# Weight conversion on three engines: a parametric relu on ScalarE, one VectorE instruction a part, V's lower half on GpSimd, and landing places inside the converted weight

## The chip, the cores and the metric

The kernel runs on one NeuronCore of one Trainium2 chip. The metric is the device time of one execution in microseconds (us). A time is given as the median of several executions. The profile is of one further execution, and its span is measured from the first to the last instruction. Engines: PE (TensorE, matmuls), PEld (its weight loads), DVE (VectorE), ACT (ScalarE), POOL (GpSimd) and SP, whose queue issues all DMAs here.

## The reference

Attention with pooled queries, then an MLP with a rational activation:

```python
# q, k, v: (4, 8, 1152, 64) float32;  w_in (512, 2048), w_out (2048, 512) float64
q_pool = q.reshape(B, H, S // 2, 2, D).mean(axis=3)          # 576 query rows
attn = softmax(scale * q_pool @ k^T)                         # 576 x 1152 per head
x = (attn @ v) laid out as (2304 tokens, 512)
h = x @ w_in
g = (a0 + a1 h + a2 h^2 + a3 h^3) / (1 + |b0| |h| + |b1| h^2 + 1e-6)
out = g @ w_out                                              # (2304, 512) float32
```

The two weights come from a random generator in float64, and nothing narrows them. The kernel therefore reads them as pairs of 32-bit words, a low word and a high word for each element, and makes float32 values of them itself. Everything is computed in pairs of float16 numbers, a high and a low part that together carry float32's precision.

## The kernel before, in words

**Attention.** A unit is a pair of heads in one batch. For each unit `prep` loads K, Q and V, finds their largest sums of squares (`pr_stat`, ACT), derives scales, and splits each operand in a high part (`pr_hi`, ACT) and a low part (`pr_lo`, DVE). V's high part is `v1`, its low part `v2`, and `v3` is a scaled copy of `v1` (`pr_v3`, DVE). K and Q are turned by a transposing DMA. A unit has nine tiles of 128 query rows. `attend` takes one tile through a fixed chain: scores on PE into the PSUM tile `sc` (`at_fill`, L718), row maxima on DVE (`at_max`, L725), their turn on PE (`at_turn`, L728), a copy of the row on ACT (`at_row`, L732), the shifted and transposed scores on PE into `st` (`at_fill2`, L741 and L742), exp on ACT (`at_exp`, L749), and the split of its result into halves on DVE (`at_split`, L757). `product` multiplies with V three tiles later (`at_pv`, L771), and `at_x` (ACT, L788) copies the result out. There are one `sc` and one `st`, so tiles follow one another closely. There are 144 tiles.

**Weights.** `weights` treats `w_in` (`wi`) and then `w_out` (`wo`) in 16 parts of 128 x 512 elements each. For every part:

- `w_load` (SP, L457) brings 512 KB of raw words into one of two buffers with the tag `raw`.
- `w_win` (POOL, L465) multiplies the high word, read as a float32, by a power of two, and writes it to `wf`, a float32 tile that holds all 16 parts.
- `w_bits` (DVE) runs three instructions: L471 moves the top three bits of the low word into the high word's place, L472 keeps only the sign of the high word, and L473 shifts `wf` left by three and ORs in these bits.
- `w_stat` (ACT, L478) sums squares.

Once all parts are there, a scale is found, and `w_hi` (ACT, L500) and `w_lo` (DVE, L504) write the two float16 parts. For `wi`, four column sums of absolute values follow (`w_abs`, `w_colsum`); they use the `raw` buffers too. When both weights are done `w_close` frees this memory and lets the first MLP chunk begin ("late").

**MLP.** A chunk is 128 tokens; 18 of them, in an order fixed by hand. `chunk` normalizes and splits the attention result; `step` does a quarter of the hidden columns: `mo_h` on PE (L913), the polynomials and the quotient on ACT, DVE and POOL (`mo_abs` L926, `mo_f` L944, `mo_e2` L948, `mo_ln` L952, `mo_rem` L971 and others), and `mo_o` on PE (L984 to L986). A chunk needs its tiles of all four units of a batch: the first chunk needs 30 tiles.

**Order.** Every operation is registered with an engine, an estimated duration in ns, a wished time and what it reads and writes. `Plan.order` runs a list scheduler forward and backward several times over these estimates and keeps the shortest result. The instructions are issued in that order, so each engine's queue has one fixed order, and an estimate that is changed can change the order of the whole program. The waits at run time are true dependences; the estimates set none.

Of the kernel before, what the change touches and what calls it, by code (L numbers as in the profile page):

```python
# [10 lines left out]
F16 = mybir.dt.float16  # L11
I32 = mybir.dt.int32
U16 = mybir.dt.uint16
BF16 = mybir.dt.bfloat16
AF = mybir.ActivationFunctionType
ALU = mybir.AluOpType
# [252 lines left out]
def kernel(  # L269
# [175 lines left out]
    def w_open():  # L445
        st["stg_cm"] = tc.tile_pool(name="stg", bufs=1)
        st["stg"] = st["stg_cm"].__enter__()

    def w_load(n, i):

        t = st["stg"].tile([P, 512, 2], I32, tag="raw", name=f"raw_{n}{i}", bufs=NRAW)
        st["raw", n, i] = t
        if n == "wi":
            src = w_in.bitcast(I32)[i // 4 * P:(i // 4 + 1) * P, (i % 4) * 1024:(i % 4 + 1) * 1024]
        else:
            src = w_out.bitcast(I32)[i * P:(i + 1) * P, :]
        nc.sync.dma_start(out=t.rearrange("p f w -> p (f w)"), in_=src)  # L457

    def w_win(n, i):
        if i == 0:
            st["wf", n] = st["stg"].tile([P, 16, 512], F32, tag="wf", name=f"wf_{n}")
        u = st["raw", n, i][:, :, 1]
        nc.gpsimd.tensor_scalar(st["wf", n][:, i, :], u.bitcast(F32), 2.0 ** -111, 1.0, ALU.mult, ALU.mult)  # L465

    def w_bits(n, i):
        mi = st["wf", n][:, i, :].bitcast(I32)
        r = st["raw", n, i]
        h = r.rearrange("p f w -> p (f w)").bitcast(U16).rearrange("p (f w) -> p f w", w=4)  # L470
        nc.vector.tensor_scalar(h[:, :, 2], h[:, :, 1], 13, None, ALU.logical_shift_right)  # L471
        nc.vector.tensor_scalar(h[:, :, 3], h[:, :, 3], 0x8000, None, ALU.bitwise_and)  # L472
        nc.vector.scalar_tensor_tensor(mi, mi, 3, r[:, :, 1], ALU.logical_shift_left, ALU.bitwise_or)  # L473

    def w_stat(n, i):

# [192 lines left out]
    def pr_lo(j, w):  # L669
        d = pairs[j]  # L670
        stt = nc.vector.scalar_tensor_tensor
        if w == "v":
            stt(pr_new(j, "v2"), d["vn"], d["ss"][:, 2:3], d["v1"][:, :, 0:D], ALU.mult, ALU.subtract)
        elif w == "q":
            stt(spq[:, KC:2 * KC, 0, :], d["qn"][:, :, 0, :], d["ss"][:, 1:2], spq[:, 0:KC, 0, :], ALU.mult, ALU.subtract)
        else:
            src = d["kn"].rearrange("p h c d -> p (h c) d")
            stt(d["spk"][:, :, 1, :], src, d["ss"][:, 0:1], d["spk"][:, :, 0, :], ALU.mult, ALU.subtract)
# [290 lines left out]
    def mo_rem(c, f):  # L969
        w = wk[c, f]  # L970
        nc.gpsimd.tensor_tensor(w["e2"], w["t"], w["e2"], ALU.subtract)  # L971
# [50 lines left out]
    def prep(j, part):  # L1022
        bb, hp, _, mode = units[j]
        o = j % 2
        if j == 0:
            at = [-100.0 + i for i in range(20)]
        else:
            p0, p1 = tile_t[first_t[j]], tile_t[first_t[j - 1]]
            sp = (p0 - p1) / 9.0
            at = [p1 + (PRM["pr0"] + PRM["pr1"] * i) * sp for i in range(20)]  # L1030
        if mode == "again":
            if hp < 2:
                for i in (0, 1) if part == 0 else (2, 3, 4):
                    add("dma", cost(256 * op_cols(i)), at[6], lambda i=i: pr_again(j, i), r=[("kept", bb, hp, i)], w=[("set", o, i)], seq=["seqag"])
                if part == 0:
                    add("dma", (625, 820, 624), at[7], lambda: pr_kb(j), r=[("set", o, 1)], w=[("set", o, 5)])
            return
        if part == 1:
            add("act", 1240, at[14], lambda: pr_hi(j, "v"), r=["vn", ("ss", j)], w=[("set", o, 2)])
            add("dve", 1500, at[15], lambda: pr_lo(j, "v"), r=["vn", ("ss", j), ("set", o, 2)], w=[("set", o, 3)])  # L1040
            add("dve", 370, at[16], lambda: pr_v3(j), r=[("set", o, 2)], w=[("set", o, 4)])
            if mode == "first" and hp < 2:
                for i in range(5):
                    add("dma", cost(256 * op_cols(i)), at[17], lambda i=i: pr_save(j, i), r=[("set", o, i)], w=[("kept", bb, hp, i)], seq=["seqsv"])
            return
        add("dma", cost(128 * 4608), at[0], lambda: pr_load_k(j), w=["kn"])
        add("dma", (1400, 1640, 449), at[0], lambda: pr_load_q(j), w=["qn"])
        add("dma", cost(128 * 4608), at[1], lambda: pr_load_v(j), w=["vn"])
        add("pool", 1500, at[6], lambda: pr_pool(j), w=["qn"])
        add("act", 1146, at[6], lambda: pr_stat(j, 0), r=["kn"], w=[("st", j), "spk"])  # L1050
        add("act", 700, at[6], lambda: pr_stat(j, 1), r=["qn"], w=[("st", j), "spk"])
        add("act", 1146, at[6], lambda: pr_stat(j, 2), r=["vn"], w=[("st", j), "spk"])
        chain(at[7], half_exp(lambda: pairs[j]["st"]), w=[("st", j)])
        bank = over_all(at[7], lambda: pairs[j]["st"], (0, 1, 2, 2), 3, [("st", j)], False)
        on_dve, on_pool = pr_scale(j)
        chain(at[7], on_dve(bank), r=["ALLB"], w=[("ss", j)], bank=B_ALL)
        chain(at[7] + 1.0, on_pool, r=[("ss", j)], w=[("esc", j)])
        for i in range(2):
            add("pool", 400, at[7] + 1.0, lambda i=i: pr_sv(j, i), r=[("ss", j)], w=[("sv", bb, hp, i)])
        for i, w in enumerate(("k", "q")):  # L1060
            add("act", 1240, at[8 + 2 * i], lambda w=w: pr_hi(j, w), r=[w + "n", ("ss", j)], w=["sp" + w])
            add("dve", 820 if w == "q" else 1650, at[9 + 2 * i], lambda w=w: pr_lo(j, w), r=[w + "n", ("ss", j)], w=["sp" + w])
            add("dma", T_TR2, at[9 + 2 * i], lambda w=w: pr_tr(j, w), r=["sp" + w], w=[("set", o, 0 if w == "q" else 1)])
            if w == "k":
                add("dma", (625, 820, 624), at[10], lambda: pr_kb(j), r=[("set", o, 1)], w=[("set", o, 5)])

    def attend(t):
        j, slot = tiles[t]
        o = j % 2
        s = time_of(t)  # L1070
        jp = prep_of[j]
        E = ("E", t % NE)
        M = ("M", t % NM)
        wide = slot == 8
        add("pe", (650, 1100) if wide else (490, 960), s, lambda: at_fill(t), r=[("set", o, 0), ("set", o, 1)], w=["S"], seq=["seqS"], bank=B_S)
        add("dve", 1330, s + 0.6, lambda: at_max(t), r=["S"], w=[M], bank=B_S)
        add("pe", (60, 128), s + 2.1, lambda: at_turn(t), r=[M], w=["TURN"], seq=["seqM"], bank=B_TURN)
        add("act", 230, s + 2.3, lambda: at_row(t), r=["TURN", ("set", o, 0)], w=[("row", t)], bank=B_TURN)
        add("pe", (1150, 2304) if wide else (1010, 2304), s + 2.7, lambda: at_fill2(t), r=[("row", t), ("set", o, 0), ("set", o, 1), ("set", o, 5)], w=["T"], seq=["seqT"], bank=B_T)
        add("act", 1300, s + 3.9, lambda: at_exp(t), r=["T", ("esc", jp)], w=[E], seq=["seqE"], bank=B_T)  # L1080
        add("dve", 780, s + 5.3, lambda: at_split(t), w=[E], seq=["seql"])

    def product(g, host):
        j, bb, hp, slot, _ = at_rows(g)
# [7 lines left out]
    def weights(n, s0):  # L1092
        for i in range(16):
            s = s0 + PRM["ws"] * i
            raw, wf = ("raw", i % NRAW), ("wf", i)
            add("dma", cost(128 * 4096), s, lambda i=i: w_load(n, i), w=[raw], seq=["raw"])
            add("pool", 700, s + 4, lambda i=i: w_win(n, i), r=[raw], w=[wf], seq=["win"])
            add("dve", 2300, s + 4, lambda i=i: w_bits(n, i), w=[wf, raw])
            add("act", 615, s + 6, lambda i=i: w_stat(n, i), r=[wf], w=[("wst", n, i)])
        s = s0 + 16 * PRM["ws"] + 2  # L1100
        add("dve", 100, s, lambda: w_max1(n), r=[("wst", n, i) for i in range(16)], w=[("m1", n)])
# [1 line left out]
        bank = over_all(s, lambda: st["m1", n], (0,), 1, [("m1", n)], True)  # L1103
        chain(s, w_scale(n, bank), r=["ph"], w=[("sw", n)])
        for i in range(8):
            wf = [("wf", 2 * i), ("wf", 2 * i + 1)]
            add("act", 1141, s + PRM["wl"] * i, lambda i=i: w_hi(n, i), r=wf + [("sw", n)], w=[(n, 0, i)])
            add("dve", 1330, s + PRM["wl"] * i, lambda i=i: w_lo(n, i), r=wf + [("sw", n), (n, 0, i)], w=[(n, 1, i)])
        s += 8 * PRM["wl"]
# [62 lines left out]
    def step(p, f):  # L1172
# [16 lines left out]
        add("pool", 1330, u + PRM["m_f"], lambda: mo_e2(c, f), r=[A], w=[E2])  # L1189
        add("act", 700, u + PRM["m_ln"], lambda: mo_ln(c, f), r=[E2], w=[A])  # L1190
        add("act", 620, u + PRM["m_ln"], lambda: mo_r(c, f), w=[A])
        add("dve", 750, u + PRM["m_ghi"], lambda: mo_ghi(c, f), r=[T, A], w=[G], seq=["seqG"])
        add("dve", 770, u + PRM["m_d1"], lambda: mo_d1(c, f), r=[G], w=[E2])
        add("pool", 1400, u + PRM["m_rem"], lambda: mo_rem(c, f), r=[T], w=[E2])
        add("dve", 800, u + PRM["m_glo"], lambda: mo_glo(c, f), r=[A], w=[G, E2, T])

        po = "po_t" if last else "po"
        wos = [("wo", l, x) for l in range(2) for x in range(8)]
# [66 lines left out]
```

## Time and profile before

| what | value |
|---|---|
| median of 3 runs (lowest, highest) | 953.59 us (952.13, 958.34) |
| profiled execution: time, span | 954.2 us, 952.4 us |
| busy: PE, DVE, ACT, POOL | 816.0, 794.1, 602.2, 446.0 us |
| mean granted TensorE clock | 0.939 |

The profiled execution takes 954.2 us with the 1.8 us around its span, and lies 0.6 us above the median. A row of the groups gives line, engine, operation, output<-input, shapes, count, then busy time and mean ns of one, then the engine's idle time just before these instructions with what ended it. A row of the windows gives the busy time of each engine in one stretch, then the granted clock and the DMA share.

### The profile page before, as it was taken

The page shows a single profiled execution, that of the slowest core. Times are in us where ns is not written, and L with a number is a line of the kernel's source. Part 1 is how long each engine was busy: PE and PEld are TensorE (multiplying, and loading weights), DVE is VectorE, ACT ScalarE, POOL GpSimd, SP SyncE. Part 2 cuts the span into 40 slices and gives each one's busy share as a digit, 9 for nine tenths or more (in the row PEclk, how much of TensorE's full clock was granted, in tenths as well). Part 3 has the DMA queues.
Part 4 walks back from the last instruction along what each step waited for, and adds up shares of the span by engine and source line. Part 5 has one row for each costly group of instructions (what it writes and reads, how often), then busy time and mean ns, then how long its engine had stood idle before and what let it go on. Part 6 is the DMA issues. An engine that isn't in the chain of part 4 may idle for free.

```text
span 952.4 us, 27847 instructions
## 1 busy us (share of the span) xinstructions
PE 816.0 (86%) x12196; PEld 650.4 (68%) x12196; DVE 794.1 (83%) x1075; ACT 602.2 (63%) x905; POOL 446.0 (47%) x482
## 2 busy tenths in 40 slices
PE   0477675545999999989998999989899998999998
PEld 0266554444877877768777788668677777887764
DVE  7698797888999897868999888869888897996765
ACT  4466595456876676657675686557667755775453
POOL 4212103342565553436764553425856544645765
PEclk9998777766999999979999999989999999999999
DMA  5784518462340060652150061445736120430100
GB/s 188 199 182 132 139 35 215 155 177 60 60 103 13 13 149 13 139 124 49 24 140 23 13 150 21 130 117 138 141 125 149 38 40 24 113 113 13 35 12 23
DMA packets 121338, 88.79 MB, mean 93 GB/s; under 512 B 96769, under 2 KB 98817, under 8 KB 121217
## 3 DMA queue, kind: packets, MB, share of 16 engines
q1 hardware_dynamic: 121216, 87.02, 37.0%
q8 instruction: 95, 1.56, 0.7%
q14 instruction: 27, 0.21, 0.1%
HBM read 49.24 MB, written 8.87 MB: 61 GB/s over the span
## 4 chain that ended last, share of the span: by engine, by line
PE 55%; DVE 12%; ACT 6%; POOL 6%; DMA 5%; issue 3%; SPq 1%; POOLq 0%; DVEq 0%; ACTq 0%
PE ph_h L913 15%; PE po L984 5%; PE po L986 5%; PE po L985 5%; PE st L741 5%; PE st L742 5%; PE sc L718 5%; PE sc L771 5%; PE st L771 4%; DVE mt L725 2%; DMA raw_wo<-in_moe_w_out_dram 2%; POOL e L944 1%; DMA k<-spk 1%; POOL e L948 1%; DVE E L757 1%
## 5 line engine op out<-in xcount | busy, mean ns | idle before, releaser
L749 ACT ACTIVATE E<-st,esc 128x1152 int32<-128x1152 f32 x144 | 188.6, 1310 | 92.4 <-PE st L728 63.0
L725 DVE TENSOR_REDUCE mt<-sc 128x1 f16<-128x1152 f32 x144 | 194.5, 1351 | 27.0 <-PE sc L718 18.9
L741 PE MATMUL st<-q,k 128*128 128x128 f16 (+1 forms) x1440 | 182.2, 224 | 34.9 <-ACT q L732 30.2
L913 PEld LDWEIGHTS <-wi 128*128 128x128 f16 x3456 | 199.9, 99 | 16.4 <-DVE t L939 9.3
L913 PE MATMUL ph_h<-x,wi 128*128 128x128 f16 x3312 | 201.9, 221 | 5.7 <-DVE t L939 5.7
L742 PE MATMUL st<-q,kb 65*128 65x128 f16 (+1 forms) x1440 | 182.7, 224 | 2.8 <-DMA kb<-k 2.8
L742 PEld LDWEIGHTS <-kb 65*128 65x128 f16 x1440 | 139.2, 103 | 49.0 <-issue 42.3
L971 POOL TENSOR_TENSOR e<-t,e 128x512 f32<-128x512 f32 x72 | 106.4, 1478 | 118.3 <-DVE e L967 108.4
L771 PEld LDWEIGHTS <-E 128*128 128x128 f16 (+1 forms) x4320 | 152.4, 105 | 12.9 <-issue 6.9
L757 DVE TENSOR_SCALAR E<-E 128x2304 f16<-128x2304 uint16 x144 | 129.8, 908 | 29.8 <-ACT E L749 29.6
L741 PEld LDWEIGHTS <-k 128*128 128x128 f16 x1440 | 139.7, 103 | 14.0 <-issue 8.8
L718 PE MATMUL sc<-k,q 128*128 128x384 f16 (+1 forms) x480 | 104.2, 354 | 42.3 <-DVE mt L725 25.6
L944 POOL TENSOR_SCALAR e<-A,b_abs 128x512 f32<-128x512 f32 x72 | 72.5, 1008 | 97.0 <-ACT A L926 97.0
L984 PE MATMUL po<-wo,g 128*128 128x512 f16 x288 | 109.2, 379 | 0.0
L986 PE MATMUL po<-wo,g 128*128 128x512 f16 x288 | 109.1, 379 | 0.0
L985 PE MATMUL po<-wo,g 128*128 128x512 f16 x288 | 109.1, 379 | 0.0
L948 POOL TENSOR_TENSOR e<-e,A 128x512 f32<-128x512 f32 x72 | 97.7, 1357 | 5.7
L718 PEld LDWEIGHTS <-q 128*128 128x128 f16 (+1 forms) x480 | 39.2, 104 | 69.2 <-issue 33.4
L952 ACT ACTIVATE A<-e,q_one 128x512 f32<-128x512 f32 x72 | 51.9, 721 | 51.7 <-POOL e L948 50.8
L926 ACT ACTIVATE A<-ph_h,cf 128x512 f32<-128x512 f32 x69 | 47.3, 686 | 58.2 <-PE ph_h L913 57.7
L975 DVE SCALAR_TENSOR_TENSOR g<-e,cf,A 128x512 f16<-128x512 f32 x72 | 63.0, 875 | 21.8 <-POOL e L971 21.7
L771 PE MATMUL sc<-v,E 128*128 128x65 f16 (+3 forms) x2160 | 80.3, 201 | 1.1 <-DVE mt L725 1.1
(126 smaller groups left out, 1212.6 us busy)
## 6 DMA issues: line engine op xcount, KB each, us to landing
kn<-in_k_dram SPq DMA_DIRECT2D x16, 576.0 KB, 4.2
vn<-in_v_dram SPq DMA_DIRECT2D x16, 576.0 KB, 5.4
qn<-in_q_dram SPq DMA_DIRECT2D x16, 512.0 KB, 4.9
raw_wi<-in_moe_w_in_dram SPq DMA_DIRECT2D x16, 512.0 KB, 5.3
raw_wo<-in_moe_w_out_dram SPq DMA_DIRECT2D x16, 512.0 KB, 3.6
kb<-k SPq DMA_DIRECT2D x18, 288.0 KB, 4.7
out_dram<-ob SPq DMA_DIRECT2D x16, 256.0 KB, 2.3
keep<-v SPq DMA_DIRECT2D x4, 292.5 KB, 6.2
```

Of the source, the lines that this page charges most:

```text
L718: nc.tensor.matmul(SC[ps, jj, 0:TH], d["q"][:, slot, ps], d["k"][:, h * KC + 3 * jj:h * KC + 3 * jj + 3, :].rearrange("p c m -> p (c m)"), ...
L725: nc.vector.tensor_reduce(mts[t % NM][:, D:D + 1], SC[:, :, 0:TH], AX.XY, ALU.max, negate=True)
L741: nc.tensor.matmul(o, d["k"][:, h * KC + c, :], d["q"][:, slot, qs], start=True, stop=False)
L742: nc.tensor.matmul(o, d["kb"][0:D + 1, h * KC + c, :], d["q"][0:D + 1, KC + slot, qs], start=False, stop=True)
L749: nc.scalar.activation(out=d["e"].rearrange("p (a c) -> p a c", a=3), in_=ST[:, :, 0:TH], func=AF.Exp, bias=esc[:, 1:2], scale=esc[:, 0:1],)
L757: nc.vector.tensor_scalar(e.bitcast(F16), e.bitcast(U16), 2.0 ** -6, None, ALU.mult)
L771: nc.tensor.matmul(pv[:, 0:w], e[:, c, qs, part], pairs[j][n_v][:, h * KC + c, :], start=(c == 0 and i == 0), stop=(c == KC - 1 and i == 2),)
L913: nc.tensor.matmul(mo[c, f]["p2"][:, i, :], wi[wl][:, kk, fs], x[:, xl * KD + kk, :], start=(n == 0), stop=(n == 3 * KD - 1))
L948: nc.gpsimd.tensor_tensor(w["e2"], w["e2"], w["A"], ALU.mult)
L984: nc.tensor.matmul(po, g[0][:, e, :], wo[0][:, kk, :], start=(kk == 0), stop=False)
L985: nc.tensor.matmul(po, g[0][:, e, :], wo[1][:, kk, :], start=False, stop=False)
L986: nc.tensor.matmul(po, g[1][:, e, :], wo[0][:, kk, :], start=False, stop=(kk == KF - 1))
```

## The change

Weight parts: `w_win` moves from POOL to ACT and becomes a parametric relu, whose slope for negative values lets the later shift leave the sign in place. A new `w_low` on POOL scales the low word, in place, as an unsigned integer to its three top bits. `w_bits` is left with one DVE instruction. Raw words of parts 2, 5 and 8 land in the last two parts of `wf` instead of a `raw` buffer. V's low part becomes two POOL instructions instead of one on DVE. Several estimates of the planner are changed.

```diff
+    IN_WF = (2, 5, 8)
     def w_load(n, i):
-        t = st["stg"].tile([P, 512, 2], I32, tag="raw", name=f"raw_{n}{i}", bufs=NRAW)
+        if i in IN_WF:
+            if ("wf", n) not in st:
+                st["wf", n] = st["stg"].tile([P, 16, 512], F32, tag="wf", name=f"wf_{n}")
+            t = st["wf", n][:, 14:16, :].bitcast(I32).rearrange("p a (f w) -> p (a f) w", w=2)
+        else:
+            t = st["stg"].tile([P, 512, 2], I32, tag="raw", name=f"raw_{n}{i}", bufs=NRAW)
...
     def w_win(n, i):
-        u = st["raw", n, i][:, :, 1]
-        nc.gpsimd.tensor_scalar(st["wf", n][:, i, :], u.bitcast(F32), 2.0 ** -111, 1.0, ALU.mult, ALU.mult)
+        u = st["raw", n, i][:, :, 1].bitcast(F32)
+        nc.scalar.activation(out=st["wf", n][:, i, :], in_=u, func=AF.Prelu, scale=2.0 ** -111, alpha=-(2.0 ** 32))
+    def w_low(n, i):
+        u = st["raw", n, i][:, :, 0].bitcast(U32)
+        nc.gpsimd.tensor_scalar(u, u, 2.0 ** -29, 7.49 / 8, ALU.mult, ALU.mult)
     def w_bits(n, i):
         mi = st["wf", n][:, i, :].bitcast(I32)
-        nc.vector.tensor_scalar(h[:, :, 2], h[:, :, 1], 13, None, ALU.logical_shift_right)
-        nc.vector.tensor_scalar(h[:, :, 3], h[:, :, 3], 0x8000, None, ALU.bitwise_and)
-        nc.vector.scalar_tensor_tensor(mi, mi, 3, r[:, :, 1], ALU.logical_shift_left, ALU.bitwise_or)
+        nc.vector.scalar_tensor_tensor(mi, mi, 3, st["raw", n, i][:, :, 0], ALU.logical_shift_left, ALU.bitwise_or)
...
         if w == "v":
-            stt(pr_new(j, "v2"), d["vn"], d["ss"][:, 2:3], d["v1"][:, :, 0:D], ALU.mult, ALU.subtract)
+            nc.gpsimd.tensor_scalar(d["vn"], d["vn"], d["ss"][:, 2:3], 1.0, ALU.mult, ALU.mult)
+            nc.gpsimd.tensor_tensor(pr_new(j, "v2"), d["vn"], d["v1"][:, :, 0:D], ALU.subtract)
...
-            add("dve", 1500, at[15], lambda: pr_lo(j, "v"), ...)
+            add("pool", 3250, at[15], lambda: pr_lo(j, "v"), ...)
-        add("dve", 780, s + 5.3, lambda: at_split(t), w=[E], seq=["seql"])
+        add("dve", 840, s + 5.3, lambda: at_split(t), w=[E], seq=["seql"])
...
+            home = sum(j not in IN_WF for j in range(i)) % NRAW
+            raw, wf = ("wf", 14) if i in IN_WF else ("raw", home), ("wf", min(i, 14))
-            add("pool", 700, s + 4, lambda i=i: w_win(n, i), r=[raw], w=[wf], seq=["win"])
-            add("dve", 2300, s + 4, lambda i=i: w_bits(n, i), w=[wf, raw])
+            add("act", 630, s + 4, lambda i=i: w_win(n, i), r=[raw], w=[wf], seq=["win"])
+            add("pool", 830, s + 4, lambda i=i: w_low(n, i), w=[("low", n, i)], r=[raw], seq=["low"])
+            add("dve", 800, s + 4, lambda i=i: w_bits(n, i), r=[raw, ("low", n, i)] if raw != wf else [("low", n, i)], w=[wf])
```

Other estimates changed: `at_max` 1330 to 1350, `at_row` 230 to 268, `pr_v3` 370 to 790, `mo_ghi` 750 to 785, `mo_d1` 770 to 830, `mo_rem` 1400 to 1460, `mo_glo` 800 to 890.

More of the change, by code (lines that the diff above doesn't have):

```diff
@@ L13 @@
 U16 = mybir.dt.uint16
+U32 = mybir.dt.uint32
 BF16 = mybir.dt.bfloat16
@@ L461, in w_win @@
     def w_win(n, i):
-        if i == 0:
+        if ("wf", n) not in st:
             st["wf", n] = st["stg"].tile([P, 16, 512], F32, tag="wf", name=f"wf_{n}")
-        u = st["raw", n, i][:, :, 1]
-        nc.gpsimd.tensor_scalar(st["wf", n][:, i, :], u.bitcast(F32), 2.0 ** -111, 1.0, ALU.mult, ALU.mult)
+        u = st["raw", n, i][:, :, 1].bitcast(F32)
[3 more added lines that the diff above has]
+        nc.gpsimd.tensor_scalar(u, u, 2.0 ** -29, 7.49 / 8, ALU.mult, ALU.mult)
     def w_bits(n, i):
         mi = st["wf", n][:, i, :].bitcast(I32)
[L469 to L473, printed above, removed]
+        nc.vector.scalar_tensor_tensor(mi, mi, 3, st["raw", n, i][:, :, 0], ALU.logical_shift_left, ALU.bitwise_or)
     def w_stat(n, i):
@@ L1039, in prep @@
             add("act", 1240, at[14], lambda: pr_hi(j, "v"), r=["vn", ("ss", j)], w=[("set", o, 2)])
-            add("dve", 1500, at[15], lambda: pr_lo(j, "v"), r=["vn", ("ss", j), ("set", o, 2)], w=[("set", o, 3)])
-            add("dve", 370, at[16], lambda: pr_v3(j), r=[("set", o, 2)], w=[("set", o, 4)])
+            add("pool", 3250, at[15], lambda: pr_lo(j, "v"), r=[("ss", j), ("set", o, 2)], w=["vn", ("set", o, 3)])
+            add("dve", 790, at[16], lambda: pr_v3(j), r=[("set", o, 2)], w=[("set", o, 4)])
             if mode == "first" and hp < 2:
@@ L1075, in attend @@
         add("pe", (650, 1100) if wide else (490, 960), s, lambda: at_fill(t), r=[("set", o, 0), ("set", o, 1)], w=["S"], seq=["seqS"], bank=B_S)
-        add("dve", 1330, s + 0.6, lambda: at_max(t), r=["S"], w=[M], bank=B_S)
+        add("dve", 1350, s + 0.6, lambda: at_max(t), r=["S"], w=[M], bank=B_S)
         add("pe", (60, 128), s + 2.1, lambda: at_turn(t), r=[M], w=["TURN"], seq=["seqM"], bank=B_TURN)
-        add("act", 230, s + 2.3, lambda: at_row(t), r=["TURN", ("set", o, 0)], w=[("row", t)], bank=B_TURN)
+        add("act", 268, s + 2.3, lambda: at_row(t), r=["TURN", ("set", o, 0)], w=[("row", t)], bank=B_TURN)
         add("pe", (1150, 2304) if wide else (1010, 2304), s + 2.7, lambda: at_fill2(t), r=[("row", t), ("set", o, 0), ("set", o, 1), ("set", o, 5)], w=["T"], seq=["seqT"], bank=B_T)
         add("act", 1300, s + 3.9, lambda: at_exp(t), r=["T", ("esc", jp)], w=[E], seq=["seqE"], bank=B_T)
-        add("dve", 780, s + 5.3, lambda: at_split(t), w=[E], seq=["seql"])
+        add("dve", 840, s + 5.3, lambda: at_split(t), w=[E], seq=["seql"])
     def product(g, host):
@@ L1094, in weights @@
             s = s0 + PRM["ws"] * i
-            raw, wf = ("raw", i % NRAW), ("wf", i)
+            home = sum(j not in IN_WF for j in range(i)) % NRAW
+            raw, wf = ("wf", 14) if i in IN_WF else ("raw", home), ("wf", min(i, 14))
             add("dma", cost(128 * 4096), s, lambda i=i: w_load(n, i), w=[raw], seq=["raw"])
-            add("pool", 700, s + 4, lambda i=i: w_win(n, i), r=[raw], w=[wf], seq=["win"])
-            add("dve", 2300, s + 4, lambda i=i: w_bits(n, i), w=[wf, raw])
+            add("act", 630, s + 4, lambda i=i: w_win(n, i), r=[raw], w=[wf], seq=["win"])
+            add("pool", 830, s + 4, lambda i=i: w_low(n, i), w=[("low", n, i)], r=[raw], seq=["low"])
+            add("dve", 800, s + 4, lambda i=i: w_bits(n, i), r=[raw, ("low", n, i)] if raw != wf else [("low", n, i)], w=[wf])
             add("act", 615, s + 6, lambda i=i: w_stat(n, i), r=[wf], w=[("wst", n, i)])
@@ L1105, in weights @@
         for i in range(8):
-            wf = [("wf", 2 * i), ("wf", 2 * i + 1)]
+            wf = [("wf", min(2 * i, 14)), ("wf", min(2 * i + 1, 14))]
             add("act", 1141, s + PRM["wl"] * i, lambda i=i: w_hi(n, i), r=wf + [("sw", n)], w=[(n, 0, i)])
@@ L1191, in step @@
         add("act", 620, u + PRM["m_ln"], lambda: mo_r(c, f), w=[A])
[L1192 to L1195, printed above, removed]
+        add("dve", 785, u + PRM["m_ghi"], lambda: mo_ghi(c, f), r=[T, A], w=[G], seq=["seqG"])
+        add("dve", 830, u + PRM["m_d1"], lambda: mo_d1(c, f), r=[G], w=[E2])
+        add("pool", 1460, u + PRM["m_rem"], lambda: mo_rem(c, f), r=[T], w=[E2])
+        add("dve", 890, u + PRM["m_glo"], lambda: mo_glo(c, f), r=[A], w=[G, E2, T])
         po = "po_t" if last else "po"
```

## The prediction

> **What bounds the kernel now.** I read the page's slices first, then the busy time by stage, then the chain of waits inside the stage that looked slow.
>
> ```profile
> PE 816.0 (86%) x12196; PEld 650.4 (68%) x12196; DVE 794.1 (83%) x1075; ACT 602.2 (63%) x905; POOL 446.0 (47%) x482
> ...
> PE   0477675545999999989998999989899998999998
> ...
> PEclk9998777766999999979999999989999999999999
> ```
>
> A slice is 23.8 us. From the third to the tenth PE is busy for 40 to 70% of each, and from the fourth the granted clock is low; from the eleventh on both are nearly full. The border is the first MLP chunk. The stages, by window; the last row counts row maxima alone (L725, one a tile) in the slow one:
>
> ```profile
> core 0: us, PE busy (x) PEld busy (x) DVE busy (x) ACT busy (x) POOL busy (x), PEclk, DMA share, GB/s
> 0.00:31.00 31.00, 1.25 (x5) 0.61 (x6) 21.12 (x41) 12.03 (x22) 11.16 (x17) 1.00 0.68 189
> 31.00:233.00 202.00, 124.64 (x1651) 100.12 (x1650) 169.16 (x241) 124.92 (x194) 50.69 (x70) 0.76 0.55 146
> 233.00:400.00 167.00, 163.56 (x2649) 133.01 (x2647) 153.17 (x190) 116.97 (x172) 82.67 (x80) 1.00 0.32 70
> 400.00:860.00 460.00, 438.55 (x6881) 354.78 (x6878) 390.59 (x525) 306.02 (x453) 244.66 (x271) 0.98 0.37 87
> 860.00:952.40 92.40, 88.01 (x1023) 61.83 (x1021) 60.09 (x81) 42.31 (x65) 56.78 (x46) 1.00 0.08 21
> ...
> 31.00:233.00 202.00, 44.69 (x34) 0.76 0.55 146
> ```
>
> After 233 us PE idles 29.3 of 719.4 us: that part is bound by PE and can hardly shrink. Before it, in what I call the head, DVE is busy 21.1 + 169.2 = 190.3 of 233 us (0.82), and PE does 124.6 x 0.76 = 95 us of full-clock work for 34 tiles, 2.8 us each, at a pace of 202 / 34 = 5.9 us. The head ends with the weights:
>
> ```profile
> 182.89 5.00 DMA raw_wo<-in_moe_w_out_dram
> 187.96 0.65 POOL wf_wo L465
> 188.63 0.74 DVE raw_wo L471
> 189.37 0.58 DVE raw_wo L472
> 189.97 0.99 DVE wf_wo L473
> ...
> 217.51 9.65 DVE wo L504 x8
> ...
> 232.79 2.26 PE ph_h L913 x38
> ```
>
> This is the chain of waits: a part's landing, then POOL, then three DVE instructions, over and over; then `w_lo`, and the first `mo_h` at 232.8. What PE waits for in the head (31 to 233 us), and after it:
>
> ```profile
> PE st L741 <- ACT q L732: 22.8, 13, 6.8
> PE sc L718 <- DVE mt L725: 17.2, 14, 2.4
> ...
> PE sc L718 <- DVE mt L725: 8.4, 9, 2.5
> PE ph_h L913 <- DVE t L939: 5.7, 7, 2.7
> ```
>
> So DVE carries the head, with ACT behind it, and a time for the change is a time for the first `mo_h`.
>
> **The change part by part.** The rows of what goes, stays and is nearest to what comes:
>
> ```profile
> L471 DVE TENSOR_SCALAR raw_wi<-raw_wi 128x512 uint16<-128x512 uint16 x16 | 12.2, 765 | 5.4 <-POOL wf_wi L465 5.4
> L471 DVE TENSOR_SCALAR raw_wo<-raw_wo 128x512 uint16<-128x512 uint16 x16 | 11.9, 746 | 4.5 <-POOL wf_wo L465 4.5
> L472 DVE TENSOR_SCALAR raw_wi<-raw_wi 128x512 uint16<-128x512 uint16 x16 | 13.0, 814 | 0.0
> L472 DVE TENSOR_SCALAR raw_wo<-raw_wo 128x512 uint16<-128x512 uint16 x16 | 12.8, 799 | 0.0
> L465 POOL TENSOR_SCALAR wf_wi<-raw_wi 128x512 f32<-128x512 f32 x16 | 13.0, 812 | 40.4 <-DMA raw_wi<-in_moe_w_in_dram 40.3
> L465 POOL TENSOR_SCALAR wf_wo<-raw_wo 128x512 f32<-128x512 f32 x16 | 12.5, 784 | 46.8 <-DMA raw_wo<-in_moe_w_out_dram 30.7 <-DVE v L682 16.1
> L478 ACT ACTIVATE wi<-wf_wi 128x512 f16<-128x512 f32 x16 | 10.0, 625 | 15.4 <-DVE wf_wi L473 15.3
> L926 ACT ACTIVATE A<-ph_h,cf 128x512 f32<-128x512 f32 x69 | 47.3, 686 | 58.2 <-PE ph_h L913 57.7
> L673 DVE SCALAR_TENSOR_TENSOR v<-vn,ss,v 128x1152 f16<-128x1152 f32 x16 | 24.7, 1543 | 0.0
> L944 POOL TENSOR_SCALAR e<-A,b_abs 128x512 f32<-128x512 f32 x72 | 72.5, 1008 | 97.0 <-ACT A L926 97.0
> L948 POOL TENSOR_TENSOR e<-e,A 128x512 f32<-128x512 f32 x72 | 97.7, 1357 | 5.7
> ```
>
> *`w_bits`.* L471 and L472 go: 12.2 + 11.9 + 13.0 + 12.8 = 49.9 us of DVE, all in the head. L473 keeps shape and stride, so its cost stays.
>
> *`w_low`* has `w_win`'s count, shape and stride; I take its 0.8 us, so POOL stays even on the weights.
>
> *`w_win` on ACT.* 32 activations of 128x512: 0.625 (L478, from SBUF) to 0.686 us (L926) each, 20.0 to 22 us; I take 20.0, the row with the same source. It adds a wait: ACT now stands until a part has landed, and `at_row` and `at_exp` queue behind it, for which PE waits. POOL waits 40.3 + 30.7 = 71 us for landings today, but with little else to do. How late POOL is for the next in line is seen in DVE's wait for it: 5.4 + 4.5 = 9.9 us. I count these 9.9 us for ACT as inside its unused share, and keep 71 us as the upper end.
>
> *Landing places.* Three of 16 loads of each weight no longer wait for a `raw` buffer. The 5.00 us of landing in the chain above would partly start earlier: nothing to 5 us for each of six loads. I put it at nothing beyond letting the parts keep up with DVE.
>
> *V's lower part.* DVE sheds 24.7 us (L673). The first row here is the part of it after the head; the others are durations at the least, the median and the most, L757's group, and `mo_o`:
>
> ```profile
> 233.00:952.40 719.40, 17.65 (x11) 0.99 0.32 74
> ...
> L944 POOL TENSOR_SCALAR e<-A,b_abs x72: 760/772/2237, 236.4 to 936.9; 128x512 f32<-128x512 f32 x72
> L948 POOL TENSOR_TENSOR e<-e,A x72: 1261/1272/2257, 237.3 to 938.7; 128x512 f32<-128x512 f32 x72
> L757 DVE TENSOR_SCALAR E<-E x144: 707/753/1960, 43.9 to 877.0; 128x2304 f16<-128x2304 uint16 x144
> ...
> L757 DVE TENSOR_SCALAR E<-E 128x2304 f16<-128x2304 uint16 x144 | 129.8, 908 | 29.8 <-ACT E L749 29.6
> L984 PE MATMUL po<-wo,g 128*128 128x512 f16 x288 | 109.2, 379 | 0.0
> ```
>
> 24.7 - 17.65 = 7.0 us are in the head. POOL pays, by elements (1152 / 512 = 2.25), 2.25 x (0.772 + 1.272) = 4.6 us a unit by medians and 2.25 x (1.008 + 1.357) = 5.3 us by means, against 3.25 in the planner: some 80 us in all. Behind them queue `mo_f`, `mo_e2` and `mo_rem`; but POOL is busy only 53% of the time after 233 us, and `mo_o`, which needs the `g` that these feed, shows no idle time of PE before it (0.0). After the head I put DVE's relief (PE's waits for DVE there, 8.4 + 5.7 = 14.1 us in the two last rows of PE's waits) against POOL's delay (at most 11 units x 5.3 = 58 us were all of it passed on) and take nothing.
>
> The L757 row shows 707 ns at best and 1960 at worst for one shape: something holds it. The Trainium skill, SBUF — State Buffer, section "SBUF: two separate sides", gives a rule that speaks against this part: VectorE and GpSimd share one port pair as an exclusive lock for a whole instruction, and the loser blocks fully. By it 32 longer POOL instructions could each hold a DVE instruction for half their 2.3 us, an estimate of 37 us on DVE, more than the 24.7 it sheds. The trace bears the mechanism out but not that size: L757's whole excess is 144 x (908 - 707) ns = 29 us at 47% POOL, which for 80 us more of POOL (8% of the span) is near 5 us.
>
> *Planner.* New estimates reorder everything. What a worse or better order is worth cannot be read off; PE's idle time after the head bounds it at -29 us, and I allow as much above.
>
> **The sum.** In the head DVE is left with 190.3 - 49.9 - 7.0 = 133.4 us; at today's share of 0.82 that is 163 us. ACT comes to 12.0 + 124.9 + 20.0 = 157 us, at the same share 192 us: ACT is what is late next. I take 200 for the first `mo_h`, 8 above ACT's figure because each tile still passes PE, DVE and ACT in turn. That is 33 us earlier. By then fewer tiles are done: the first chunk needs 30, so I take 31 for 34, and 3 x 2.8 = 8.4 us of PE work move behind the border. 33 - 8.4 = 24: 954.2 - 24 = 930 us, and the 0.6 us to the median is nothing beside this.
>
> **The rivals.**
>
> *More than that (13%).* ACT reaches over 0.9 of its time and the head ends near DVE's figure, at 175 to 180 with 30 tiles: 55 - 11 = 44 us, 910; with PE's waits for DVE after the head gone too, 900. Against it: ACT also carries `at_row`, the longest wait of PE above.
>
> *Gain lost to order and latency (18%).* The head's tiles keep their pace because the chain through one `sc` and one `st` and the serial run of `wi`, column sums, `wo` set it: the first `mo_h` comes at 220 to 230, and the time is 945 to 957. For it: ACT stays 59% busy in the head today and PE still waits on its row copy. Against: DVE's busy share.
>
> *ACT held by landings (10%), slower.* If ACT's queue stands for most of POOL's 71 us, its head demand is 157 + 71 = 228 us, at 0.82 278: the first `mo_h` comes 45 us later, some eight tiles more are done by then (22 us), and the time is 977. It decides from 191 - 157 = 34 us of holding, since 191 / 0.82 = 233. For it: ACT is the engine of every tile's chain. Against: the 9.9 us.
>
> *It doesn't run as written (4%).* If the parametric relu needed another function table than exp, each of 32 would bring two loads:
>
> ```profile
> L417 ACT ACT_TABLE_LOAD x1 | 1.3, 1283 | 0.7 <-PEq L1249 0.7
> ```
>
> 64 x 1.28 = 82 us on ACT, hence 239 / 0.82 = 291 us for the head and about 985. One load serves all functions today.
>
> **How the numbers follow.** The forecast, 917 to 944, has 55%. Runs of this kernel differ so that about 1% (9.5 us) is what can be told from no change: 944 and 963. Faster: 55 + 13 = 68%; within: 18%; slower: 14%. Leaving out the 14% and the lowest tip, the range goes from 904 to 958.
>
> **What would show it.** The uint16 groups vanish; DVE falls to 794 - 75 = 720 us, ACT rises to 622, POOL to about 525. The first `ph_h` matmul comes near 200, with a granted clock in the head above 0.76; after it PE idles about 30 us as now. The forecast is wrong if the parametric relu has long idle time before it ended by the `raw` DMA with `at_exp` late behind it, if the first `ph_h` is near 230, or if PE begins to wait for `g`.

## The result, and the profile after

The changed kernel takes 929.03 us (median of 4; 928.07 to 932.57) against 952.86 us for the kernel before (median of 4; 950.86 to 958.34). The ratio is 0.9748, 95% interval 0.9699 to 0.9797. The profiled execution takes 928.07 us with a span of 926.3 us.

The first lines of the page after, beside those of before:

```profile
span 926.3 us, 27847 instructions
...
PE 807.9 (87%) x12196; PEld 641.9 (69%) x12196; DVE 764.8 (83%) x995; ACT 621.4 (67%) x937; POOL 507.4 (55%) x514
...
PE   0586876669899999899899999879899998999997
...
PEclk9979796969999999799999999999999999999999
```

PE's full stretch begins a slice earlier. The border is the first `mo_h` (its line is now L924), from the timelines of before and after. Below them are the windows on both sides of it, then the head for row maxima (one a tile) alone, then the stretch after the border for the products with V (30 matmuls a tile; L771, now L782) alone, first before, then after:

```profile
232.72 2.88 PE L913 MATMUL ph_h<-x,wi 128*128 128x128 f16 x48
0.00:232.72 232.72, 125.61 (x1650) 100.45 (x1651) 190.10 (x281) 136.69 (x216) 61.85 (x87) 0.79 0.56 152
232.72:952.40 719.68, 690.40 (x10547) 549.91 (x10546) 604.02 (x794) 465.56 (x690) 384.11 (x395) 0.99 0.32 74
0.00:232.72 232.72, 44.51 (x33) 0.79 0.56 152
232.72:952.40 719.68, 117.25 (x3456) 113.24 (x3456) 0.99 0.32 74
```

```profile
198.41 4.08 PE L924 MATMUL ph_h<-x,wi 128*128 128x128 f16 x48
0.00:198.41 198.41, 120.02 (x1687) 94.27 (x1688) 152.78 (x218) 158.44 (x255) 76.13 (x97) 0.86 0.69 178
198.41:926.30 727.89, 687.87 (x10510) 547.63 (x10509) 612.03 (x778) 462.93 (x682) 431.30 (x417) 0.99 0.32 74
0.00:198.41 198.41, 50.04 (x37) 0.86 0.69 178
198.41:926.30 727.89, 116.45 (x3456) 112.08 (x3456) 0.99 0.32 74
```

The columns are the window, its length, then busy time of PE, PEld, DVE, ACT and POOL (in the rows of one line only of the engine that runs it), granted clock, DMA share and GB/s. The head is 34.3 us shorter, although 37 row maxima instead of 33 fall in it. But the stretch after the border is 8.2 us *longer*. The four row maxima more don't mean four tiles less to do there: only the first scores run ahead, the products with V lie as before (3456 of their 4320 matmuls after the border in both), and PE's busy time after it falls by 2.5 us only. What grows is PE's idle time, from 719.7 - 690.4 = 29.3 to 727.9 - 687.9 = 40.0 us, by 10.7 us. DVE is busy 8 us longer there although V's lower part has left it, and POOL 47 us longer.

The groups after of what was moved or is new:

```profile
L475 ACT ACTIVATE wf_wi<-raw_wi 128x512 f32<-128x512 f32 x13 | 8.7, 668 | 2.1 <-DMA raw_wi<-in_moe_w_in_dram 1.9
L475 ACT ACTIVATE wf_wo<-raw_wo 128x512 f32<-128x512 f32 x13 | 8.7, 669 | 1.2 <-DMA raw_wo<-in_moe_w_out_dram 1.0
L479 POOL TENSOR_SCALAR raw_wi<-raw_wi 128x512 uint32<-128x512 uint32 x13 | 10.6, 813 | 28.2 <-DMA raw_wi<-in_moe_w_in_dram 28.2
L684 POOL TENSOR_TENSOR v<-vn,v 128x1152 f16<-128x1152 f32 x16 | 39.7, 2480 | 1.3
L683 POOL TENSOR_SCALAR vn<-vn,ss 128x1152 f32<-128x1152 f32 x16 | 24.2, 1515 | 29.0 <-ACT v L670 17.2 <-PE ph_w L346 5.7 <-issue 3.3
L418 ACT ACT_TABLE_LOAD x1 | 1.3, 1283 | 0.7 <-PEq L1262 0.7
```

The parametric relu (L475) takes 0.67 us and hardly waits for landings; the POOL instruction beside it (L479) still does the waiting. DVE waits 11.3 us for it in all, against 9.9 us for L465 before. There is one table load. V's lower part costs POOL 2.48 + 1.52 = 4.0 us a unit.

### The profile page after: what moved, and what is told of

Its sections match the earlier page's. It is cut to its first block, busy times and chain, and to the rows that moved or that the text cites. A ratio compares the mean times of both kernels' runs of the same rounds, so it can differ in the third digit from the quotient of the medians.

```text
span 926.3 us, 27847 instructions
## 1 busy us (share of the span) xinstructions
PE 807.9 (87%) x12196; PEld 641.9 (69%) x12196; DVE 764.8 (83%) x995; ACT 621.4 (67%) x937; POOL 507.4 (55%) x514
## 4 chain that ended last, share of the span: by engine, by line
PE 53%; DVE 20%; ACT 9%; DMA 7%; issue 5%; POOL 3%; SPq 2%; POOLq 0%; DVEq 0%; ACTq 0%
PE ph_h L924 15%; PE st L752 5%; PE st L753 5%; PE sc L729 5%; PE sc L782 5%; PE po L995 4%; PE po L997 4%; PE po L996 4%; PE st L782 4%; DVE mt L736 4%; DVE E L768 3%; ACT E L760 3%; DVE g L974 2%; DVE t L950 2%; DVE g L986 2%
## 5 line engine op out<-in xcount | busy, mean ns | idle before, releaser
L924 PEld LDWEIGHTS <-wi 128*128 128x128 f16 x3456 | 202.8, 100 | 24.7 <-DVE t L950 16.4
L924 PE MATMUL ph_h<-x,wi 128*128 128x128 f16 x3312 | 204.2, 222 | 12.9 <-DVE t L950 12.7
L752 PE MATMUL st<-q,k 128*128 128x128 f16 (+1 forms) x1440 | 178.1, 221 | 23.1 <-ACT q L743 19.3
L753 PE MATMUL st<-q,kb 65*128 65x128 f16 (+1 forms) x1440 | 178.7, 221 | 2.8 <-DMA kb<-k 2.8
L753 PEld LDWEIGHTS <-kb 65*128 65x128 f16 x1440 | 136.7, 101 | 35.7 <-issue 28.2
L782 PEld LDWEIGHTS <-E 128*128 128x128 f16 (+1 forms) x4320 | 146.3, 103 | 14.6 <-issue 8.6
L768 DVE TENSOR_SCALAR E<-E 128x2304 f16<-128x2304 uint16 x144 | 138.1, 965 | 21.4 <-ACT E L760 21.1
L752 PEld LDWEIGHTS <-k 128*128 128x128 f16 x1440 | 137.0, 102 | 22.1 <-issue 15.9
L955 POOL TENSOR_SCALAR e<-A,b_abs 128x512 f32<-128x512 f32 x72 | 76.7, 1066 | 117.1 <-ACT A L937 117.0
L986 DVE SCALAR_TENSOR_TENSOR g<-e,cf,A 128x512 f16<-128x512 f32 x72 | 69.7, 971 | 14.3 <-POOL e L982 14.3
L782 PE MATMUL sc<-v,E 128*128 128x65 f16 (+3 forms) x2160 | 77.7, 198 | 1.7 <-DVE mt L736 1.5
```

Source lines behind the costliest of these rows:

```text
L752: nc.tensor.matmul(o, d["k"][:, h * KC + c, :], d["q"][:, slot, qs], start=True, stop=False)
L753: nc.tensor.matmul(o, d["kb"][0:D + 1, h * KC + c, :], d["q"][0:D + 1, KC + slot, qs], start=False, stop=True)
L768: nc.vector.tensor_scalar(e.bitcast(F16), e.bitcast(U16), 2.0 ** -6, None, ALU.mult)
L782: nc.tensor.matmul(pv[:, 0:w], e[:, c, qs, part], pairs[j][n_v][:, h * KC + c, :], start=(c == 0 and i == 0), stop=(c == KC - 1 and i == 2),)
L924: nc.tensor.matmul(mo[c, f]["p2"][:, i, :], wi[wl][:, kk, fs], x[:, xl * KD + kk, :], start=(n == 0), stop=(n == 3 * KD - 1))
```

## The experiments

**V's lower part, in one fixed order.** Three kernels keep the changed kernel's order exactly (the planner is told the same), and differ only in what is issued at the place of V's lower part. With the changed kernel they make a square: POOL's two instructions there or not, DVE's one there or not. In `v_both` POOL's two write a scratch tile that nobody reads; in `v_neither` V's lower part is zero, so the product lacks that term.

```diff
 # v_dve_same_order: DVE alone
-            nc.gpsimd.tensor_scalar(d["vn"], d["vn"], d["ss"][:, 2:3], 1.0, ALU.mult, ALU.mult)
-            nc.gpsimd.tensor_tensor(pr_new(j, "v2"), d["vn"], d["v1"][:, :, 0:D], ALU.subtract)
+            stt(pr_new(j, "v2"), d["vn"], d["ss"][:, 2:3], d["v1"][:, :, 0:D], ALU.mult, ALU.subtract)
 # v_both: the same, and before it
+            nc.gpsimd.tensor_scalar(vdumh, d["vn"], d["ss"][:, 2:3], 1.0, ALU.mult, ALU.mult)
+            nc.gpsimd.tensor_tensor(vdumh, d["vn"], d["v1"][:, :, 0:D], ALU.subtract)
 # v_neither: instead of all
+            nc.vector.memset(pr_new(j, "v2"), 0.0)
```

> The changed kernel in exactly its own order, but V's lower part is again one DVE instruction, issued at the place where the two POOL instructions stood. Theory (lock): after the first MLP matmul the changed kernel loses time because long POOL instructions hold the DVE; with V back on DVE the glo, d1, split and v3 groups fall to their means of before (875, 830, 908, 456 ns), POOL loses 64 us, and the time falls by 5 to 15 us to 914 to 924 us, with the first ph_h still within 3 us of 198. Rival (order): the loss comes from the order alone, which is unchanged here: 926 to 932 us. Second rival (DVE relief): V's 24.7 us on DVE hurt more than the holding did: 932 to 940 us.

> The changed kernel in its own order, with V's lower part on DVE (one instruction) and two POOL instructions of the same size in front of it that write a scratch tile nobody reads. Against V on DVE alone in the same order (920.5 us) it adds only POOL's occupation: about 64 us of it. Theory (the POOL instructions cost, by holding DVE and by delaying what queues on POOL): 927 to 940 us, with split, d1 and glo on DVE at or above the changed kernel's means (965, 925, 971 ns). Rival (the 9 us come from the dependence of v2 on a late POOL, which the scratch does not have): 918 to 924 us.

> The changed kernel in its own order, with V's lower part left out: v2 is only zeroed, so the product lacks that term. This takes the two POOL instructions away and leaves DVE some 0.6 us instead of 1.5 a unit. Theory (POOL's occupation costs 9 us, DVE's own 24 us next to nothing because DVE has idle time): 916 to 921 us, within 4 us of V on DVE in the same order. Rival (DVE is as short as PE after the border, so its 15 us count): 906 to 914 us.

| median us | DVE's instruction left out | DVE's instruction there |
|---|---|---|
| no POOL instructions | 914.79 (`v_neither`) | 920.49 (`v_dve_same_order`) |
| POOL's two | 929.03 (the changed kernel) | 949.73 (`v_both`) |

Ratios to the kernel before, in the order of the table's rows: 0.9587 (0.9538 to 0.9637), 0.9644 (0.9594 to 0.9693), 0.9748 and 0.9952 (0.9922 to 0.9982). DVE's own instruction costs 5.7 us over the 0.54 us memset in its place, between the two theories' ranges; the runs of these two kernels overlap (911.9 to 918.3 and 915.8 to 923.4 us), so it is a rough number. POOL's two cost 14.2 us where DVE has none, so the move loses 8.5 us. Together they cost 35 us, far over the expectation. The groups of the DVE instructions, first of the changed kernel:

```profile
L768 DVE TENSOR_SCALAR E<-E 128x2304 f16<-128x2304 uint16 x144 | 138.1, 965 | 21.4 <-ACT E L760 21.1
L986 DVE SCALAR_TENSOR_TENSOR g<-e,cf,A 128x512 f16<-128x512 f32 x72 | 69.7, 971 | 14.3 <-POOL e L982 14.3
L974 DVE SCALAR_TENSOR_TENSOR g<-t,cf,A 128x512 f16<-128x512 f32 x72 | 62.5, 868 | 13.6 <-ACT A L967 10.3 <-PE po L996 3.1
L693 DVE TENSOR_SCALAR v<-v 128x1170 f16<-128x1170 f16 x16 | 13.7, 859 | 0.1
...
L768 DVE TENSOR_SCALAR E<-E x144: 707/752/2853, 39.5 to 848.3; 128x2304 f16<-128x2304 uint16 x144
```

Then `v_dve_same_order`, with its page's busy line:

```profile
PE 803.0 (88%) x12196; PEld 637.3 (70%) x12196; DVE 758.9 (83%) x1011; ACT 621.4 (68%) x937; POOL 442.4 (48%) x482
...
L767 DVE TENSOR_SCALAR E<-E 128x2304 f16<-128x2304 uint16 x144 | 124.6, 872 | 22.0 <-ACT E L759 21.8
L985 DVE SCALAR_TENSOR_TENSOR g<-e,cf,A 128x512 f16<-128x512 f32 x72 | 66.6, 927 | 13.8 <-POOL e L981 13.8
L973 DVE SCALAR_TENSOR_TENSOR g<-t,cf,A 128x512 f16<-128x512 f32 x72 | 59.9, 831 | 11.3 <-ACT A L966 7.6 <-PE po L995 3.4
L683 DVE SCALAR_TENSOR_TENSOR v<-vn,ss,v 128x1152 f16<-128x1152 f32 x16 | 23.6, 1474 | 1.7 <-ACT v L670 1.5
L692 DVE TENSOR_SCALAR v<-v 128x1170 f16<-128x1170 f16 x16 | 12.2, 764 | 0.0
...
L767 DVE TENSOR_SCALAR E<-E x144: 706/753/1837, 39.3 to 838.7; 128x2304 f16<-128x2304 uint16 x144
```

And V's own instruction in `v_both`, where it stands beside POOL's two:

```profile
L685 POOL TENSOR_TENSOR vdumh<-vn,v 128x1152 f16<-128x1152 f32 x16 | 45.6, 2849 | 19.4 <-ACT v L671 18.5
L686 DVE SCALAR_TENSOR_TENSOR v<-vn,ss,v 128x1152 f16<-128x1152 f32 x16 | 34.5, 2159 | 1.9 <-ACT v L671 1.7
```

This is the reading that matters most here. Off DVE goes an instruction group of 23.6 us; yet DVE is busy 758.9 us with it and 764.8 us without it. So 23.6 + 5.9 = 29.5 us come back as longer times of DVE instructions that are otherwise the same, in the same order: the split (`E<-E`) alone 13.5 us. `v_neither` says the same: DVE is busy 744.8 us there, 8.6 of them in the 16 memsets, so 764.8 - 736.2 = 28.6 us come with POOL's two. The split's median stays (752 and 753 ns), its longest goes from 1837 to 2853 ns, and in `v_both` V's instruction goes from 1474 to 2159 ns. So single instructions are held; the work as such is not slower. The expectation was missed in one point: only the split fell below its mean of before (872 for 908 ns), while glo (L985, 927 for 875 ns), v3 (L692, 764 for 456) and d1 (904 for 830) stay above theirs with V on DVE too, so POOL's pair isn't all that lengthens them. The rival by which order made the loss falls for these 8.5 us, since the order is the same. The same stretch past the border, with the same matmuls, is in `v_dve_same_order`:

```profile
199.29:916.80 717.51, 681.98 (x10510) 542.26 (x10509) 605.94 (x789) 463.08 (x682) 386.27 (x395) 1.00 0.32 75
```

That is 10.4 us less than the changed kernel's 727.9. Of these 4.5 us are idle time of PE (40.0 against 35.5) and 5.9 us are busy time for the same 10510 matmuls, at a granted clock of 0.99 against 1.00; why the clock was granted lower isn't shown. What part comes from DVE held and what part from the queue on POOL, the square doesn't separate. Two idle rows of PE and one of ACT past the border are below, after and then `v_dve_same_order`:

```profile
PE ph_h L924 <- DVE t L950: 12.7, 9, 4.2
...
PE po L997 <- DVE g L986: 2.2, 2, 1.4
...
ACT A L963 <- POOL e L959: 47.3, 38, 3.3
```

```profile
PE ph_h L923 <- DVE t L949: 7.9, 9, 2.4
...
PE po L996 <- DVE g L985: 2.3, 2, 1.4
...
ACT A L962 <- POOL e L958: 41.3, 35, 3.3
```

PE's wait for `t`, which ACT and DVE make without POOL, grew; its wait for `g`, which POOL feeds, did not, and DVE's own wait for POOL before `g` hardly did (13.8 and 14.3 us above). That speaks for DVE held. But ACT waits 6 us longer for POOL's `e`, and the next `t` queues behind that on ACT, so that POOL's delay isn't excluded.

**V's move by itself.** The kernel before, with only this part of the change (and its two estimates):

```diff
-            stt(pr_new(j, "v2"), d["vn"], d["ss"][:, 2:3], d["v1"][:, :, 0:D], ALU.mult, ALU.subtract)
+            nc.gpsimd.tensor_scalar(d["vn"], d["vn"], d["ss"][:, 2:3], 1.0, ALU.mult, ALU.mult)
+            nc.gpsimd.tensor_tensor(pr_new(j, "v2"), d["vn"], d["v1"][:, :, 0:D], ALU.subtract)
```

> The kernel before with V's lower part alone moved to POOL, planned at 3250 ns (v3 at 790). Theory (the move is a loss of some 8 us that the weight part covered; in the head it takes 7 us from the engine that is short there): 952 to 964 us. Rival (DVE bound the head, so there the move is a gain): 940 to 950 us.

970.52 us, ratio 1.0175 (1.0122 to 1.0228): a loss of 17 us, more than the theory gave. The rival is out: not even in the head, where DVE was short, does the move gain (first `mo_h` at 234.1 against 232.7 us). Here the order is a new one too, so the 17 us are not the move's alone.

**The other way round: all of the change but V's move, with the planner told.**

```diff
+            add("dve", 1500, at[15], lambda: pr_lo(j, "v"), r=["vn", ("ss", j), ("set", o, 2)], w=[("set", o, 3)])
+            add("dve", 370, at[16], lambda: pr_v3(j), r=[("set", o, 2)], w=[("set", o, 4)])
```

> The changed kernel with V's lower part on DVE and the planner told so (1500 ns on DVE, v3 at 370). Theory (lock): the weight part carries the whole gain, so first ph_h at 196 to 206 us and a time of 912 to 926 us, below the changed kernel. Rival (V's move is part of the gain, by 7 us in the head and 18 us after it): 932 to 945 us.

916.99 us, ratio 0.9606 (0.9564 to 0.9649), first `mo_h` at 198.1 us. So the rest of the change, with its landing places and estimates, carries the whole gain without V's move.

**The estimates alone**, in the kernel before (so also those of the row maximum, its row and the four steps of the MLP):

```diff
-        add("dve", 780, s + 5.3, lambda: at_split(t), w=[E], seq=["seql"])
+        add("dve", 840, s + 5.3, lambda: at_split(t), w=[E], seq=["seql"])
```

> The kernel before with only the planner's new durations (row maximum, row copy, split, ghi, d1, rem, glo); no instruction differs, only their order. Theory: order alone is worth less than 1%: 943 to 962 us. Rival (planner): the better durations carry much of the gain: 930 to 942 us.

950.0 us, ratio 0.9949 (0.9926 to 0.9972), first `mo_h` at 231.8 us: 0.5%, and 0.9 us of it in the head.

**Landing places.** The changed kernel without them, and two kernels with V's lower part on DVE and more of them:

```diff
 # no_in_wf
-    IN_WF = (2, 5, 8)
+    IN_WF = ()
 # v_dve_wf4, v_dve_wf5, both on v_dve_replanned
+    IN_WF = (2, 5, 8, 11)
+    IN_WF = (2, 5, 8, 11, 13)
```

> The changed kernel with all raw parts landing in the two raw buffers, none in the converted weight. Prediction's step: landing places are worth nothing beyond letting the parts keep up: first ph_h within 5 us of 198, time 927 to 935 us. Rival: with the DVE short, the buffer cycle (landing near 4 to 5 us plus 2 us of work, two buffers) is what paces the parts, 3.3 us each instead of 2.6 over two times nine parts: first ph_h 8 to 15 us later, time 935 to 943 us.

> V's lower part on DVE and planned so (917.0 us with three landing places in the converted weight), with part 11 landing there too. Theory (landings paced the weights: without the three places the time was 939, with them 929): one more of each weight is worth 2 to 6 us: 911 to 916 us, first ph_h 2 to 7 us before 198. Rival (with three places the parts are no longer paced by landings): 915 to 920 us.

> V's lower part on DVE and five landing places in the converted weight (2, 5, 8, 11, 13) for four (914.0 us). Theory (landings still pace the parts): 908 to 913 us. Rival (with three or four places they no longer do; what is left is order): 911 to 920 us.

Without any: 939.16 us, ratio 0.9841 (0.9796 to 0.9887), 10 us slower than with three. With four and V on DVE 913.97 us (ratio 0.9578, 0.9535 to 0.962), with five 909.01 us (0.9533, 0.9504 to 0.9562), where three gave 916.99. The issues of the `w_in` and the `w_out` parts on SP (durations in ns at the least, the median and the most, then the first and the last start in us), of before, of `no_in_wf` and of the changed kernel (whose other three of each go to `wf`, in between):

```profile
L457 SPq DMA_DIRECT2D raw_wi<-in_moe_w_in_dram x16: 327/334/530, 3.6 to 104.6; - x16
L457 SPq DMA_DIRECT2D raw_wo<-in_moe_w_out_dram x16: 327/328/475, 143.0 to 200.0; - x16
```

```profile
L466 SPq DMA_DIRECT2D raw_wi<-in_moe_w_in_dram x16: 327/328/741, 3.6 to 80.3; - x16
L466 SPq DMA_DIRECT2D raw_wo<-in_moe_w_out_dram x16: 327/335/1171, 129.1 to 183.5; - x16
```

```profile
L466 SPq DMA_DIRECT2D raw_wi<-in_moe_w_in_dram x13: 327/333/576, 3.6 to 75.4; - x13
L466 SPq DMA_DIRECT2D raw_wo<-in_moe_w_out_dram x13: 327/328/1062, 121.1 to 166.5; - x13
```

From the first to the last of sixteen `w_out` parts are 57.0, 54.4 and 45.4 us: 3.8, 3.6 and 3.0 us a part. With DVE relieved but two buffers only, these come hardly faster than before; it takes the third place to make use of DVE's time. The `w_in` parts are another case: 101.0, 76.7 and 71.8 us, so there most of the gain comes with two buffers. The first `mo_h` comes at 218.8 us without the places and at 198.4 us with them, 20.4 us apart, which is more than the rival's 8 to 15 us and far over the 3.6 us by which order alone moves it (next). Of the total time 10 us are left of that, close to what order alone can do.

So the rival was right about the time of `no_in_wf`. For the other two kernels the steps of the time, 3 and 5 us, go the way of the theory, but the first `mo_h` of `v_dve_wf4` comes at 203.1 us, 5 us later than with three places, where 2 to 7 us earlier was expected; that of `v_dve_wf5` comes at 195.8 us. Each step is also within what order alone moves. So what a fourth and a fifth place are worth isn't shown. `v_dve_wf5` is the fastest version found.

**Which engine the head waits for now**, and how far order moves the time. One more instruction for each weight part on ACT, or one on DVE, and the changed kernel with another patience of the planner:

```diff
 # act_plus
+        nc.scalar.activation(out=st["wf", n][:, i, :], in_=st["wf", n][:, i, :], func=AF.Copy)
 # dve_plus
+        nc.vector.scalar_tensor_tensor(mi, mi, 0, mi, ALU.logical_shift_left, ALU.bitwise_or)
 # order_pat210
-    pat=180, ...
+    pat=210, ...
```

> The changed kernel with one more ACT activation a weight part, a copy of the converted part onto itself, known to the planner: 32 x 0.63 = 20 us more on ACT, all before the first MLP matmul. Theory (ACT is what is late next in the head, in use 0.80 of its time): first ph_h 15 to 25 us later than 198, time 936 to 948 us. Rival (latency and landings pace the head, engines have room): first ph_h within 8 us of 198, time 927 to 935 us.

> The changed kernel with one more DVE instruction a weight part, a shift by nothing and OR of the converted part with itself, known to the planner: 32 x 0.69 = 22 us more on DVE before the first MLP matmul. Theory (DVE no longer sets the head): first ph_h less than 8 us later than 198, time 927 to 936 us, well under the ACT twin. Rival (DVE at 0.77 of its time is as short as ACT): first ph_h 15 to 25 us later, time 936 to 950 us.

> The changed kernel with nothing altered but the planner's patience (210 for 180 ns), which gives another order of the same instructions. It shows how far order alone moves the time. Theory: less than 1%, 920 to 938 us. Rival (the measured total owes much to a lucky order): over 938 us.

Medians: 942.7 us (ratio 0.9878, 0.9843 to 0.9913 against before), 938.21 us (0.9831, 0.9806 to 0.9856) and 937.88 us (0.9833, 0.9788 to 0.9878). The heads of the first two, and the first `mo_h` of all three:

```profile
209.30 4.85 PE L927 MATMUL ph_h<-x,wi 128*128 128x128 f16 x48 [0.16 <-PE st L742]
0.00:209.30 209.30, 125.68 (x1662) 101.01 (x1663) 151.14 (x219) 173.50 (x282) 74.90 (x98) 0.78 0.61 169
```

```profile
209.67 3.70 PE L928 MATMUL ph_h<-x,wi 128*128 128x128 f16 x48
0.00:209.67 209.67, 125.15 (x1727) 101.47 (x1727) 172.87 (x245) 157.86 (x251) 83.20 (x97) 0.81 0.61 168
```

```profile
201.96 2.72 PE L924 MATMUL ph_h<-x,wi 128*128 128x128 f16 x24 [1.10 <-DMA x<-xs]
```

20 us more on ACT and 24 us more on DVE (by their groups) both move the border by 11 us. Neither theory had 11 us, and they had ACT and DVE apart: the head is not ACT's alone. Both engines are in use for about 0.8 of it (0.80 and 0.77 in the changed kernel), and each costs about half of what is put on it. And order alone, with no instruction changed, costs 8.9 us, 3.6 of them in the head. So a difference under some 9 us between kernels of different order says nothing about an instruction; this takes the times of these two, 14 and 9 us above the changed kernel, close to that limit too.

## Why the prediction was right, point by point

The time was 929.03 us for 930 forecast, inside 917 to 944. The head came out as forecast, 34 us shorter for 33. That the rest fits so closely is luck: the sum took 8.4 us off the gain for tiles that would move behind the border, and they did not; 8.2 us were lost behind it for another reason.

- *What bounds the kernel*: right, but not all of it. The 49.9 us of L471 and L472 were taken off the head's busiest engine, and the border moved from 232.7 to 198.4 us, forecast 200. With two buffers alone (`no_in_wf`) it came at 218.8 us, so the change without its landing places gives 14 of these 34 us. That is close to the 220 to 230 us of the rival by which the gain is lost to order and latency.
- *ACT in the head*: right. 158.4 us for 157; the relu 0.67 us for 0.625. The wait for landings was 1.9 + 1.0 us in the two large groups, against 9.9 allowed and 34 needed by the slower rival. That rival is out, and so is the one on function tables.
- *"At the same share 192 us: ACT is what is late next"*: the figure came out, its reason did not. `act_plus` and `dve_plus` moved the border alike. 0.80 is a share at which this head runs, with two engines in use alike, and not ACT's limit.
- *"I take 31 for 34" tiles*: wrong. Counted alike, 37 row maxima instead of 33 fall before the border, and the products with V lie where they did. The term was 8.4 us of PE's work more behind the border; PE's busy time there fell by 2.5 us.
- *Landing places at nothing "beyond letting the parts keep up with DVE"*: not priced. Letting them keep up is worth 20 us of the head and some 10 us of the time (939 to 929). The sum took the head's pace from DVE's and ACT's busy time alone and left the cycle of the buffers out: with DVE relieved, two buffers still gave 3.6 us for 3.8 us a part of `w_out`, and 5.1 for 6.7 us of `w_in`.
- *"After the head ... take nothing"*: wrong. PE idles 10.7 us more there. The sum set DVE's relief against POOL's delay, but DVE was not relieved: it is busy 612.0 us behind the border, 604.0 before. With V on DVE in the changed kernel's order the stretch takes 717.5 us, 2.2 us less than before, so V's move can account for nearly all of the loss (10.4 us there, 8.5 us of the medians). The new order is in the comparison with before as well, and no run takes it out. The sign "if PE begins to wait for `g`" did come, with 2.2 us in two waits (none before), but it is there with V on DVE too (2.3 us).
- *The port lock at 5 us*: mis-sized. DVE's instructions grew by 29.5 us. The prediction's estimate by the Trainium skill (SBUF — State Buffer, "SBUF: two separate sides": an exclusive lock for the whole instruction) was 37 us, and the measured 29.5 us agree with that far better than with 5 us. The 5 us came from the mean excess of the split alone, scaled by POOL's share; the split alone grew by 13.5 us, and 16 us came in other DVE instructions, for which the sum had no term. POOL's new instructions are also up to 1.8 times as long as those behind that excess (2.48 for 1.36 us), and the longest hold of the split grew with them (1837 to 2853 ns). Of the 45 us by which DVE (764.8) lies above the forecast 720, these are 29.5; the other 15 are there with V on DVE too (758.9, where 794.1 - 49.9 = 744.2 would be left), and why stays open.
- *POOL at 525*: 507.4; V's pair took 4.0 us a unit, under both of its prices (4.6 and 5.3). Scaling by elements was too dear: from 512 to 1152 elements the medians go from 0.77 to 1.36 us and from 1.27 to 2.49 us (the second pair also differs in types). An estimate from these four is that 0.3 us of each instruction don't grow with its elements.
- *The planner*: a bound of 29 us was allowed; 0.5% (estimates) and 1% (patience) were seen.

## What to carry to other kernels

When an instruction moves from VectorE to GpSimd, look whether VectorE's sum of busy time falls by what was moved, not whether the group is gone: here it rose by 5.9 us. When a change relieves the engine that paced a pipeline, work out the next pace, that of buffers and landings, before it is counted at nothing. And where a scheduler orders the program, first measure how far order alone moves the time, and hold the order fixed for any comparison finer than that.

## What the runs showed of the hardware that was not expected

DVE's busy time did not fall when 23.6 us of work left it; 29.5 us came back in other instructions, with an unchanged median of the split (752 ns). With one DVE instruction beside two POOL instructions that read the same operands, 73 us of POOL work whose results nobody reads cost 29 us of total time (920.5 to 949.7). And with the same 10510 matmuls behind the border, PE was busy 5.9 us longer in the changed kernel than with V on DVE in the same order, at a granted clock of 0.99 against 1.00.
